# A pooled-attention and expert-choice kernel: the low-part product of each expert's first 256 tokens folded into a 512-column product

## The chip, the cores and the metric

The kernel runs on one core of one Trainium2 chip. The metric is device time in microseconds (us) of one execution; lower is better. Where the text gives a stage or a wait, it comes from one execution taken with the hardware profiler. The engines are called as in the profile: PE is TensorE's multiplication, PEld its weight load, ACT ScalarE, DVE VectorE, POOL GpSimd and SP SyncE, which here issues loads.

## The reference

Attention with pooled keys and values gives 4608 tokens of 512 numbers. Each token then goes to one of 8 experts: tokens and experts are matched greedily by gate value, every expert taking exactly 576 tokens. An expert multiplies by w1 (512 by 1024), takes the maximum with 0, and multiplies by w2 (1024 by 512):

```python
order = np.argsort(-flat)                 # gate values of all tokens and experts
for idx in order:
    tok, e = (int(idx) // E, int(idx) % E)
    if assigned[tok] >= 0 or counts[e] >= cap:
        continue
    assigned[tok] = e
    counts[e] += 1
...
for e in range(E):
    mask = assigned == e
    h = np.maximum(x[mask] @ w1[e], 0.0)
    out[mask] = h @ w2[e]
```

Everything is float32.

## The kernel before, in words

Attention comes first and takes about a quarter of the time; the change does not touch it. Then the experts come one after the other, numbered 0 to 7 here in the order in which they are worked on. While PE works on expert e, the routing (on DVE, with small products on PE) finds the tokens of the expert that comes next, POOL gathers their rows (`xg`, line 1037), and SP loads their weights.

**Products in parts.** PE multiplies float32 numbers in a reduced form, "fp32r". To keep accuracy each factor is cut into a high part and a low part: `high1` (line 1045) copies w1 to `w1h` on ACT, `low1` (line 1049) subtracts on DVE and writes `w1l`; `high2` and `low2` (lines 1055 and 1058) do this for w2, in eight pieces each. Tokens are turned by PE in five tiles of 128, 128, 128, 128 and 64 (`xt`, line 1069, written to PSUM as `tp`); ACT copies the high part `xh` (line 1071) and DVE subtracts to get `xl` (line 1073). A product is then the sum of three: high by high, low by high, high by low.

**Stage 1** (`stage1`) takes the 576 tokens in two parts, the first 256 and the last 320. For each part there are 8 groups, one per 128 columns of w1, called f0 to f7 here. A group is 12 matmuls into one PSUM bank (line 1093): four of w1h by xh, four of w1l by xh, four of w1h by xl. Then ACT writes the high part of the maximum with 0 (`hh`, line 1098), and DVE reads the bank and `hh` and writes the low part (`hl`, line 1101). After that the bank is free. Five banks called `h` go round. Expert 0 takes its parts in halves: f0 to f3 of both parts, then f4 to f7 of both.

**Stage 2** (`products`, line 1127) multiplies hh and hl with w2h and w2l, four tiles of 128 tokens, 24 matmuls of 512 columns each; ACT copies each result to `yt` (line 1141) and POOL scatters its rows to the output (line 1107). The last 64 tokens are multiplied in plain float32 (line 1132), copied to `yh` (line 1145), and scattered as half rows ("halves"). `yh` is a tile of 128 by 256 with two buffers that take turns.

**The order of the work** on every engine is written out by a small planner in `experts` (lines 1202 to 1420). `now` counts PE's time by what the stages yield, `dve` what DVE has been given. `later(after, t, f)` puts DVE work into a list that is written out when `now` has reached the given time; `step` writes one step of the routing; `turn` turns a tile of tokens; `w1.by` and `w2.by` write the pieces of the weights. Each engine then works strictly through its own list. A small product of the routing stands between the large matmuls, at the place where the planner expects its input from DVE: if DVE is later than planned, PE waits there. Expert e+1's first two tiles must be turned before its stage 1 begins.

Of the kernel before, what the change touches and what calls it, by code (L numbers as in the profile page):

```python
# [9 lines left out]
F32 = mybir.dt.float32  # L10
F32R = mybir.dt.float32r
# [3 lines left out]
AF = mybir.ActivationFunctionType  # L15
OP = mybir.AluOpType
# [5 lines left out]
class Attention:  # L22
# [270 lines left out]
    def norm(self, i):  # L293
        c0, c1 = (i // 4 * 4, i // 4 * 4 + 4) if i < self.nt - 4 else (i, i + 1)
        rinv = self.gates(i, c0, c1)
        xt = self.wk.tile([128, 8, 64], F32, name="xt", bufs=8)
        self.nc.vector.tensor_tensor(xt, self.sums_of(i)[:, :, :64], rinv[:, :, None].to_broadcast([128, 8, 64]),
                                     op=OP.mult)
        self.store(i, xt)

    def store(self, i, xt):
        self.nc.scalar.dma_start(self.xd[128 * i:128 * i + 128], xt.rearrange("p h d -> p (h d)"))
# [681 lines left out]
class Experts:  # L984
# [75 lines left out]
    def xt(self, t, name="tp", bufs=2, later=lambda after, t, f: f()):  # L1060

        nc = self.nc
        n = min(128, self.cap - 128 * t)
        if t == 0:
            self.xh = self.buf("xh", [128, 4, 576], F32R)
            self.xl = self.buf("xl", [128, 4, 576], F32R)
        ps = self.psA.tile([128, 4, 128], F32, name=name, bufs=bufs)
        for j in range(4):
            nc.tensor.transpose(ps[:, j, :n], self.xg[:n, t, 128 * j:128 * j + 128], self.ident[:n, :n])  # L1069
        o = slice(128 * t, 128 * t + n)  # L1070
        nc.scalar.activation(self.xh[:, :, o], ps[:, :, :n], AF.Copy)  # L1071
        xl, xh = self.xl[:, :, o], self.xh[:, :, o].bitcast(F32)
        later(1.3, 0.65, lambda: nc.vector.tensor_tensor(xl, ps[:, :, :n], xh, op=OP.subtract))  # L1073

    def stage1(self, later=lambda after, t, f: f(), halves=False, bank=("h", 5)):

        nc = self.nc
        hr = self.buf("hr", [128, 8, 64])
        hh = self.buf("hh", [128, 8, 576], F32R)
        hl = self.buf("hl", [128, 8, 576], F32R)  # L1080
        self.hr, self.hh, self.hl = hr, hh, hl
        cols = slice(0, 256), slice(256, 576)
        for o, some in ((cols[0], range(4)), (cols[1], range(4)), (cols[0], range(4, 8)), (cols[1], range(4, 8))) if (
                halves) else ((cols[0], range(8)), (cols[1], range(8))):
            m = o.stop - o.start
            dt = m / 2400 + 0.017
            for f in some:
                ps = self.psA.tile([128, 512], F32, name=bank[0], bufs=bank[1])
                n = 0
                for a, b in ((self.w1h, self.xh), (self.w1l, self.xh), (self.w1h, self.xl)):  # L1090
                    for j in range(4):
                        fs = slice(128 * f, 128 * f + 128)
                        nc.tensor.matmul(ps[:, :m], a[:, j, fs], b[:, j, o], start=(n == 0), stop=(n == 11))  # L1093
                        n += 1
                        if n < 12:
                            yield dt
                yield dt
                nc.scalar.activation(hh[:, f, o], ps[:, :m], AF.Relu)  # L1098
                if o.start:
                    nc.scalar.activation(hr[:, f], ps[:, 256:320], AF.Relu)  # L1100
                later(0.65, 0.4, lambda f=f, o=o, m=m, ps=ps: nc.vector.scalar_tensor_tensor(  # L1101
                    hl[:, f, o], ps[:, :m], 0.0, hh[:, f, o].bitcast(F32), op0=OP.max, op1=OP.subtract))

    def scatter(self, rows, idx, y):
        nc = self.nc
# [96 lines left out]
def experts(ctx, tc, g, R, xd, w1, w2, out, ident, cap, keep):  # L1202
# [3 lines left out]
    nc = tc.nc  # L1206
    wk = ctx.enter_context(tc.tile_pool(name="moe", bufs=2))
    psB = ctx.enter_context(tc.tile_pool(name="psB", bufs=1, space=PSUM))
    X = Experts(tc, wk, psB, xd, w1, w2, out, ident, cap)

    toks, since, pieces, turned = {}, {}, {}, {}
    held, waiting = [], []

    lows = 0
# [3 lines left out]
    now, dve, ready = 0.0, 0.0, 0.0  # L1218

    def later(after, t, f):  # L1220

        waiting.append((now + after, t, f))

    def flush(left=0):
        nonlocal dve
        while len(waiting) > left:
            due, t, f = waiting.pop(0)
            f()
            dve = max(dve, due) + t
# [33 lines left out]
    def advance(e, t, quiet=False):  # L1263

        nonlocal now, fresh
        now += t
        fresh = False
        while True:
            if waiting and waiting[0][0] <= now:
                flush(len(waiting) - 1)  # L1270
            elif ready > now or quiet or first(e) or not step(e):
                break

    def due(e, what, t):
        return (e, what) in since and now >= since[e, what] + t

    class Pieces:
# [25 lines left out]
    def later_low(after, t, f):  # L1303
# [7 lines left out]
        lows += 1  # L1311
        later(after, t, g)

    def first(e):

        if lows:
            return True
        return e in toks and e in pieces and pieces[e].l < 4 and due(e, "id", 9)

    def turn(e, t, name="tp", bufs=2):  # L1320

        nonlocal now
        now = max(now, since[e, "rows"] + 6.0 + 1.3 * t) + 0.45
        flush(1)
        X.xt(t, name, bufs, later_low)
        turned[e] = t + 1

        if (e, t) == (0, 2):
            later(1.0, 0.2, lambda: X.load_1(behind(0), 2, 4))
        elif (e, t) == (0, 4):  # L1330
            later(1.0, 0.2, lambda: X.load_2(behind(1)))

    def turns(e, upto, late):

        nonlocal last
        t = turned.get(e, 5)
        if t < upto and due(e, "rows", 6.5 + 1.3 * t) and now >= last + 1.4 and (fresh or through or t < late):
            last = now
            turn(e, t)
# [27 lines left out]
    now, ready, dve = 0.0, 0.0, 2.5  # L1367
    last = 0.0
    for e in range(8):
        more = e < 7  # L1370
        if e:
            X.load_2(eids[e])
        w1 = pieces[e]
        w2 = Pieces(e, X.high2, X.low2)
        for n, dt in enumerate(X.stage1(later, not e)):
            k = n if e else n - 48
            if 0 <= k < 48 and n % 2:
                w1.by(4 + (k + 2) // 8)
            if not e and 2 <= n < 96:
                turns(e, 5, 5)  # L1380
            if n == (84 if e else 40):
                for t in range(turned[e], 5):
                    turn(e, t)
            if n >= 64 and n % 2:
                w2.by((n - 70) // 14 if n > 70 else 0)
            if not more and n == 48:
                assert next(g, None) is None
                flag = R.suspect()
                keep()
            elif not more and n == 56:  # L1390
                nc.gpsimd.drain()
            elif not more and n == 136:
                flag = nc.values_load(flag[0:1, 0:1], min_val=0, max_val=1)
            advance(min(e + 1, 7), dt)
            if e and n < 96:
                turns(e, 5, 3 + (n - 14) // 24)
        while w2.l < 8:
            w2.next()
        w1 = pieces[e + 1] = Pieces(e + 1, X.high1, X.low1)
        for n, dt in enumerate(X.stage2(e, *toks[e], range(5 if more else 1))):  # L1400

            advance(min(e + 1, 7), dt, n >= 96)
            if more and due(e + 1, "id", 9):
                w1.by((n - 60) // 12 if n > 60 else 0)
            if more:
                turns(e + 1, 3, (n - 52) // 12)
        if more:
            while e + 1 not in toks:
                now = max(now, ready)
                step(e + 1)  # L1410
            while w1.l < 4:
                w1.next()
            for t in range(turned[e + 1], 2):
                turn(e + 1, t)
        flush(2)
    flush()
    ps = psB.tile([128, 512], F32, name="h", bufs=5)
# [85 lines left out]
```

## Time and profile before

| | us |
|---|---|
| median of 3 runs (612.05 to 612.61) | 612.23 |
| the profiled execution, whole | 612.35 |
| its span, first to last instruction | 609.9 |
| start of stage 1 of expert 0 | 157.1 |
| expert 4: first part of stage 1 | 386.70 to 400.07 |
| expert 4: second part of stage 1 | 400.07 to 415.04 |
| expert 4: stage 2 | 415.04 to 443.26 |

In the views, L1093 is line 1093 of the kernel. A row of a group gives engine, operation, what is written and read, shape and count, then busy time and the mean length of one in ns, then the idle time before it and who ended that. A row of the timeline begins with the start and the length in us. In a row of the windows, each engine's busy time in that stretch is followed by the number of its instructions.

### The profile page before, as it was taken

To read this page: it belongs to the slowest core of one execution; us is meant where nothing else is said; L and a number is where in the kernel's file an instruction comes from. 1 tells how busy PE (TensorE), PEld (TensorE's weight loads), DVE (VectorE), ACT (ScalarE), POOL (GpSimd) and SP (SyncE) were. 2 spreads that over 40 slices of the span, in tenths; PEclk is the share of its full clock that TensorE was granted. 3 is DMA by queue.
4 is the path that set the end of the run, shared out by engine and by line. 5 is a ranking of instruction groups with operands and counts; after the bars stand their busy time and mean duration, and the time that the engine had idled before them with its cause. 6 is when DMAs were issued, how large, how long until landed. Compare 5 with 4: busy or idle time off the path is not lost.

```text
span 609.9 us, 11520 instructions
## 1 busy us (share of the span) xinstructions
PE 591.5 (97%) x4340; PEld 518.3 (85%) x4340; DVE 396.1 (65%) x1164; ACT 240.0 (39%) x562; POOL 177.3 (29%) x222
## 2 busy tenths in 40 slices
PE   8999999985999999999999999999999999999996
PEld 5999999983797799779977987898799889888975
DVE  7578888987885778767964976487367328503500
ACT  7444444461461434233432452255135325513411
POOL 2999999001200500420312301130221123011012
PEclk9999999995999999999999999999999999999999
DMA  8999972223531740616403701540081037014011
GB/s 353 419 420 423 397 274 82 77 100 98 167 116 31 254 147 22 213 62 219 134 35 116 284 1 52 207 174 18 36 323 57 34 120 278 2 52 166 1 40 43
DMA packets 32641, 92.23 MB, mean 151 GB/s; under 512 B 3488, under 2 KB 3488, under 8 KB 29888
## 3 DMA queue, kind: packets, MB, share of 16 engines
q1 hardware_dynamic: 21296, 62.92, 27.5%
q0 software_dynamic: 5952, 19.01, 9.2%
q10 hardware_dynamic: 5328, 9.48, 4.1%
q8 instruction: 35, 0.57, 0.4%
q14 instruction: 30, 0.25, 0.1%
HBM read 72.53 MB, written 18.87 MB: 150 GB/s over the span
## 4 chain that ended last, share of the span: by engine, by line
PE 81%; issue 7%; DVE 4%; DMA 3%; POOL 3%; ACT 1%; SPq 0%; POOLq 0%; ACTq 0%; another core or an unknown queue 0%; DVEq 0%
PE h L1093 32%; PE h L1127 25%; PE psa L272 6%; PE pss L227 5%; PE h L1132 4%; PE tp L1069 3%; DMA rawk<-in_k_dram 2%; PE pse L256 2%; PE rt L256 1%; PE rt L668 1%; DMA out_dram<-yt,rows 1%; PE rt L630 1%; DMA xg<-xd,rows 1%; PE rt L217 1%; DVE e L238 1%
## 5 line engine op out<-in xcount | busy, mean ns | idle before, releaser
L1127 PE MATMUL h<-w2l,hh 128*128 128x512 f32 x256 | 101.8, 398 | 0.0
L1127 PE MATMUL h<-w2h,hh 128*128 128x512 f32 x256 | 101.4, 396 | 0.3 <-PEq L1193 0.3
L1127 PE MATMUL h<-w2h,hl 128*128 128x512 f32 x256 | 101.5, 396 | 0.0
L1107 POOL DMA_INDIRECT out_dram<-yt,rows x29 | 30.3, 1045 | 232.3 <-ACT yt L1141 231.9
L1098 ACT ACTIVATE hh<-h 128x320 fp32r<-128x320 f32 (+1 forms) x128 | 52.5, 410 | 106.6 <-PE h L1093 103.3
L1093 PE MATMUL h<-xh,w1h 128*128 128x320 f32 (+1 forms) x512 | 93.2, 301 | 0.2 <-ACT xh L1071 0.2
L1093 PE MATMUL h<-xl,w1h 128*128 128x320 f32 (+1 forms) x512 | 93.4, 300 | 0.0
L1101 DVE SCALAR_TENSOR_TENSOR hl<-h,hh 128x320 fp32r<-128x320 f32 (+1 forms) x128 | 57.2, 451 | 53.1 <-ACT hh L1098 34.6
L1093 PE MATMUL h<-xh,w1l 128*128 128x320 f32 (+1 forms) x512 | 91.0, 298 | 0.0
L1093 PEld LDWEIGHTS h<-xh,w1h 128*128 128x128 f32 x512 | 75.7, 190 | 3.4 <-issue 2.7
L1093 PEld LDWEIGHTS h<-xl,w1h 128*128 128x128 f32 x512 | 76.1, 190 | 0.4
L1093 PEld LDWEIGHTS h<-xh,w1l 128*128 128x128 f32 x512 | 75.8, 189 | 0.0
L1037 POOL DMA_INDIRECT xg<-xd,rows x40 | 39.3, 982 | 101.9 <-DVE halves L806 52.7
L1141 ACT ACTIVATE yt<-h 128x512 f32<-128x512 f32 x32 | 19.1, 598 | 112.1 <-PE h L1127 67.4
L272 PE MATMUL psa<-vblk,eT 128*128 128x146 f32 (+3 forms) x390 | 59.9, 302 | 0.2
L1127 PEld LDWEIGHTS h<-w2h,hh 128*128 128x128 f32 x256 | 48.2, 188 | 9.3 <-issue 0.7
L1127 PEld LDWEIGHTS h<-w2l,hh 128*128 128x128 f32 x256 | 48.3, 189 | 8.8
L1127 PEld LDWEIGHTS h<-w2h,hl 128*128 128x128 f32 x256 | 48.2, 188 | 8.8
L272 PEld LDWEIGHTS psa<-vblk,eT 128*128 128x128 f32 (+1 forms) x390 | 50.9, 180 | 1.8 <-issue 0.3
L1049 DVE TENSOR_TENSOR w1l<-raw,w1h 128x512 fp32r<-128x512 f32 x64 | 41.7, 685 | 13.4 <-ACT w1h L1045 13.1
L1073 DVE TENSOR_TENSOR xl<-tp,xh 128x512 fp32r<-128x512 f32 (+1 forms) x40 | 25.3, 633 | 37.4 <-ACT xh L1071 37.3
L1058 DVE TENSOR_TENSOR w2l<-raw,w2h 128x512 fp32r<-128x512 f32 x64 | 43.2, 682 | 2.0 <-ACT w2h L1055 1.8
(224 smaller groups left out, 903.3 us busy)
## 6 DMA issues: line engine op xcount, KB each, us to landing
raw<-in_moe_w_dram SPq DMA_DIRECT2D x64, 512.0 KB, 6.3
xd<-xt ACTq DMA_DIRECT2D x36, 256.0 KB, 5.6
rawv<-in_v_dram SPq DMA_DIRECT2D x7, 1280.0 KB, 14.1
rawk<-in_k_dram SPq DMA_DIRECT2D x7, 1152.0 KB, 11.7
rawq<-in_q_dram SPq DMA_DIRECT2D x7, 1152.0 KB, 11.8
rawk<-in_k_dram SPq DMA_DIRECT2D x2, 576.0 KB, 4.7
rawv<-in_v_dram SPq DMA_DIRECT2D x1, 768.0 KB, 8.0
rawq<-in_q_dram SPq DMA_DIRECT2D x1, 640.0 KB, 9.0
```

The lines of the kernel that those rows point to most:

```text
L227: nc.tensor.matmul(ps[cols, j // 2, 144 * (j % 2):144 * (j % 2) + 144], self.q_of(b, j, n, cols.stop - cols.start), self.kblk[b % 4][:, j] ...
L272: self.nc.tensor.matmul(o[h], self.eT[i][:, c, h], self.vblk[b % 4][:, self.BLOCKS[c]:self.BLOCKS[c + 1]], start=(c == cs[0]), stop=(c == ...
L1037: nc.gpsimd.indirect_dma_start(out=self.xg[:n, t, :], out_offset=None, in_=self.xd, in_offset=bass.IndirectOffsetOnAxis(ap=rows[:n, t:t + ...
L1049: self.nc.vector.tensor_tensor(l, raw, h.bitcast(F32), op=OP.subtract)
L1058: self.nc.vector.tensor_tensor(self.w2l[:, i], self.raw2[e][:, i], self.w2h[:, i].bitcast(F32), op=OP.subtract)
L1073: later(1.3, 0.65, lambda: nc.vector.tensor_tensor(xl, ps[:, :, :n], xh, op=OP.subtract))
L1093: nc.tensor.matmul(ps[:, :m], a[:, j, fs], b[:, j, o], start=(n == 0), stop=(n == 11))
L1098: nc.scalar.activation(hh[:, f, o], ps[:, :m], AF.Relu)
L1101: later(0.65, 0.4, lambda f=f, o=o, m=m, ps=ps: nc.vector.scalar_tensor_tensor(hl[:, f, o], ps[:, :m], 0.0, hh[:, f, o].bitcast(F32), op0= ...
L1107: st = nc.gpsimd.indirect_dma_start(out=rows, out_offset=bass.IndirectOffsetOnAxis(ap=idx, axis=0), in_=y, in_offset=None)
L1127: nc.tensor.matmul(ps, a[:, f, o], b[:, f], start=(f == 0 and k == 0), stop=(f == 7 and k == 2))
L1132: nc.tensor.matmul(ps[64 * a:64 * a + 64, :256], self.hr[:, f], self.raw2[e][:, f, 256 * a:256 * a + 256], start=(f == 0), stop=(f == 7))
```

## The change

In the first 256 tokens' part, the high and the low part of x now stand side by side in one tile, `xa`, with 4 by 2 by 256 columns; the other 320 tokens are in `xb`. A group of the first part is 8 matmuls instead of 12 (`first`): four of w1l by the high part, 256 columns, then four of w1h by high and low side by side, 512 columns. The bank's left half then holds w1l by xh plus w1h by xh, its right half w1h by xl. The halves are added afterwards: ACT copies the right half to a tile called `yh`, DVE adds it to the left half in place, ACT takes the maximum with 0 (`hh`), and DVE makes `hl` as before. The second part (`second`) does what it did.

Since the 5th matmul of the first group already reads the low part, `lowered` writes out the subtraction of x's low parts ahead of it.

```diff
@@ xt
+            self.xa = self.buf("xa", [128, 4, 2, 256], F32R)
+            self.xb = self.buf("xb", [128, 2, 4, 320], F32R)
...
+        xh, xl = (self.xa[:, :, i, o] if t < 2 else self.xb[:, i, :, o] for i in range(2))
+        nc.scalar.activation(xh, ps[:, :, :n], AF.Copy)
+        later(1.3, 0.65, lambda: nc.vector.tensor_tensor(xl, ps[:, :, :n], xh.bitcast(F32), op=OP.subtract))
@@ stage1
-                for a, b in ((self.w1h, self.xh), (self.w1l, self.xh), (self.w1h, self.xl)):
-                    for j in range(4):
-                        fs = slice(128 * f, 128 * f + 128)
-                        nc.tensor.matmul(ps[:, :m], a[:, j, fs], b[:, j, o], start=(n == 0), stop=(n == 11))
...
+                yield from (self.second if o.start else self.first)(f, o, ps, later, ready)
+
+    def first(self, f, o, ps, later, ready):
...
+        for j in range(4):
+            nc.tensor.matmul(ps[:, :256], self.w1l[:, j, fs], self.xa[:, j, 0], start=(j == 0), stop=False,
+                             skip_group_check=True)
+            yield 0.12
+        if f == 0:
+            ready()
+        for j in range(4):
+            nc.tensor.matmul(ps, self.w1h[:, j, fs], self.xa[:, j].rearrange("p v c -> p (v c)"), start=False,
+                             stop=(j == 3), skip_group_check=True)
+            yield 0.1135
+            yield 0.1135
+        part, whole = self.wk.tile([128, 256], F32, name="yh", bufs=2), ps[:, :256]
+        nc.scalar.activation(part, ps[:, 256:], AF.Copy)
+
+        def add():
+            nc.vector.tensor_tensor(whole, whole, part, op=OP.add)
+            nc.scalar.activation(hh, whole, AF.Relu)
+            later(0.65, 0.4, lambda: nc.vector.scalar_tensor_tensor(hl, whole, 0.0, hh.bitcast(F32), op0=OP.max,
+                                                                    op1=OP.subtract))
+
+        later(0.65, 0.4, add)
@@ experts
+    def lowered():
+        while lows:
+            flush(len(waiting) - 1)
...
-        for n, dt in enumerate(X.stage1(later, not e)):
+        for n, dt in enumerate(X.stage1(later, not e, ready=lowered)):
```

The planner writes everything in another order with this, on all engines. Three places matter here. In these rows "waits" names the counters that the instruction waits for: those called DMASW count the landing of transfers that POOL issued.

**ACT at the start of expert 7.** Before, from the copy of the scattered half rows (L1145, or L1170 after) on:

```order
L1145 ACTIVATE yh<-h 128x256 [waits PE_49]
L1071 ACTIVATE xh<-tp 128x4x128 [waits PE_49]
L1071 ACTIVATE xh<-tp 128x4x64 [waits PE_49]
L1098 ACTIVATE hh<-h 128x256 [waits DVE_49,PE_49]
L1098 ACTIVATE hh<-h 128x256 [waits PE_49] x4
```

After:

```order
L1170 ACTIVATE yh<-h 128x256 [waits PE_49]
L1072 ACTIVATE xb<-tp 128x4x128 [waits PE_49]
L1072 ACTIVATE xb<-tp 128x4x64 [waits PE_49]
L1105 ACTIVATE yh<-h 128x256 [waits PE_49]
L1109 ACTIVATE hh<-h 128x256 [waits DVE_49]
L1105 ACTIVATE yh<-h 128x256 [waits DMASW4_49,PE_49,Activation_49]
L1109 ACTIVATE hh<-h 128x256 [waits DVE_49]
L1105 ACTIVATE yh<-h 128x256 [waits PE_49,Activation_49]
```

Each group now has two instructions on ACT instead of one, and the second group's copy waits for a transfer that POOL issued: the copies share the two buffers of `yh` with the half rows that are being scattered.

**DVE in the first part of expert 7**, where one small step of the routing's last test (L892) stands among the groups. Before:

```order
L1073 TENSOR_TENSOR xl<-tp,xh 128x4x128 [waits Activation_49]
L1073 TENSOR_TENSOR xl<-tp,xh 128x4x64 [waits Activation_49]
L1101 SCALAR_TENSOR_TENSOR hl<-h,hh 128x256 [waits Activation_49] x3
L892 TENSOR_SCALAR rc<-bad 128x1
L895 TENSOR_SCALAR flag<-rt 1x1 [waits PE_49]
```

After:

```order
L1108 TENSOR_TENSOR h<-h,yh 128x256 [waits DVE_49,Activation_49]
L1110 SCALAR_TENSOR_TENSOR hl<-h,hh 128x256 [waits Activation_49]
L1108 TENSOR_TENSOR h<-h,yh 128x256 [waits Activation_49]
L1110 SCALAR_TENSOR_TENSOR hl<-h,hh 128x256 [waits Activation_49]
L1108 TENSOR_TENSOR h<-h,yh 128x256 [waits Activation_49]
L1110 SCALAR_TENSOR_TENSOR hl<-h,hh 128x256 [waits Activation_49]
L892 TENSOR_SCALAR rc<-bad 128x1
L895 TENSOR_SCALAR flag<-rt 1x1 [waits PE_49]
```

The step stands behind three groups, as before, but each is now an addition and a subtraction, and both wait for ACT. On PE the product that reads `rc` (L894) stands behind the first matmul of f4 in both kernels.

**DVE at the start of expert 2**, the last pieces of the weights' low part (L1049). Before, they stand ahead of all of the expert's groups:

```order
L1049 TENSOR_TENSOR w1l<-raw_3295,w1h 128x512 [waits DMAHW3_49]
L1049 TENSOR_TENSOR w1l<-raw_3295,w1h 128x512 [waits Activation_49]
L672 TENSOR_TENSOR diagc<-rt,dq 128x32 [waits PE_49]
L676 TENSOR_REDUCE cnt<-diagc 128x8 [waits DVE_49]
L1073 TENSOR_TENSOR xl<-tp,xh 128x4x128 [waits Activation_49]
L687 TENSOR_TENSOR g_247<-rt,need_3469 32x8 [waits PE_49]
L1073 TENSOR_TENSOR xl<-tp,xh 128x4x64 [waits Activation_49]
L1101 SCALAR_TENSOR_TENSOR hl<-h,hh 128x256 [waits Activation_49]
```

After:

```order
L1108 TENSOR_TENSOR h<-h,yh 128x256 [waits Activation_49]
L1110 SCALAR_TENSOR_TENSOR hl<-h,hh 128x256 [waits Activation_49]
L625 TENSOR_TENSOR cmp<-q16a,j_196 128x1152 [waits DVE_49]
L1108 TENSOR_TENSOR h<-h,yh 128x256 [waits Activation_49]
L1110 SCALAR_TENSOR_TENSOR hl<-h,hh 128x256 [waits Activation_49]
L1049 TENSOR_TENSOR w1l<-raw_3370,w1h 128x512
L1108 TENSOR_TENSOR h<-h,yh 128x256 [waits Activation_49]
```

The eighth piece now stands behind the additions and subtractions of f0 and f1. PE reads it in the fourth matmul of f4.

More of the change, by code (lines that the diff above doesn't have):

```diff
@@ L1064, in xt @@
         if t == 0:
-            self.xh = self.buf("xh", [128, 4, 576], F32R)
-            self.xl = self.buf("xl", [128, 4, 576], F32R)
+            self.xa = self.buf("xa", [128, 4, 2, 256], F32R)
+            self.xb = self.buf("xb", [128, 2, 4, 320], F32R)
         ps = self.psA.tile([128, 4, 128], F32, name=name, bufs=bufs)
@@ L1069, in xt, with stage1 @@
             nc.tensor.transpose(ps[:, j, :n], self.xg[:n, t, 128 * j:128 * j + 128], self.ident[:n, :n])
[L1070 to L1075, printed above, removed]
+        o = slice(128 * (t % 2), 128 * (t % 2) + 128) if t < 2 else slice(128 * t - 256, 128 * t - 256 + n)
+        xh, xl = (self.xa[:, :, i, o] if t < 2 else self.xb[:, i, :, o] for i in range(2))
+        nc.scalar.activation(xh, ps[:, :, :n], AF.Copy)
+        later(1.3, 0.65, lambda: nc.vector.tensor_tensor(xl, ps[:, :, :n], xh.bitcast(F32), op=OP.subtract))
+    def stage1(self, later=lambda after, t, f: f(), halves=False, bank=("h", 5), ready=lambda: None):
         nc = self.nc
@@ L1084, in stage1 @@
                 halves) else ((cols[0], range(8)), (cols[1], range(8))):
-            m = o.stop - o.start
-            dt = m / 2400 + 0.017
             for f in some:
                 ps = self.psA.tile([128, 512], F32, name=bank[0], bufs=bank[1])
-                n = 0
-                for a, b in ((self.w1h, self.xh), (self.w1l, self.xh), (self.w1h, self.xl)):
-                    for j in range(4):
-                        fs = slice(128 * f, 128 * f + 128)
[L1093 to L1102, printed above, removed]
+                yield from (self.second if o.start else self.first)(f, o, ps, later, ready)
@@ new lines, in first @@
+    def first(self, f, o, ps, later, ready):
+        nc, hh, hl = self.nc, self.hh[:, f, o], self.hl[:, f, o]
+        fs = slice(128 * f, 128 * f + 128)
+        for j in range(4):
[17 more added lines that the diff above has]
+        later(0.65, 0.4, add)
@@ new lines, in second @@
+    def second(self, f, o, ps, later, ready):
+        nc, hh, hl = self.nc, self.hh[:, f, o], self.hl[:, f, o]
+        fs = slice(128 * f, 128 * f + 128)
+        for n, (a, b) in enumerate(((self.w1h, 0), (self.w1l, 0), (self.w1h, 1))):
+            for j in range(4):
+                nc.tensor.matmul(ps[:, :320], a[:, j, fs], self.xb[:, b, j], start=(n == j == 0),
+                                 stop=(n == 2 and j == 3))
+                yield 0.15
+        nc.scalar.activation(hh, ps[:, :320], AF.Relu)
+        nc.scalar.activation(self.hr[:, f], ps[:, 256:320], AF.Relu)
+        later(0.65, 0.4, lambda: nc.vector.scalar_tensor_tensor(hl, ps[:, :320], 0.0, hh.bitcast(F32), op0=OP.max,
+                                                                op1=OP.subtract))
```

## The prediction, as it was put on record

> **What bounds the kernel now.** First the page: its span, the engines' busy time and the chain that ended last.
>
> ```profile
> span 609.9 us, 11520 instructions
> PE 591.5 (97%) x4340; PEld 518.3 (85%) x4340; DVE 396.1 (65%) x1164; ACT 240.0 (39%) x562; POOL 177.3 (29%) x222
> PE 81%; issue 7%; DVE 4%; DMA 3%; POOL 3%; ACT 1%; SPq 0%; POOLq 0%; ACTq 0%; another core or an unknown queue 0%; DVEq 0%
> ```
>
> PE is busy in 97% of the span and holds 81% of the chain: less work on PE shortens the time, a new wait on PE lengthens it. DVE has 35% to spare, but an average hides the stages. So next the windows (length, then busy time of PE, PEld, DVE, ACT, POOL, then PE's granted clock): expert 0's halves of 256 and of 320 tokens, expert 4's first part, second part and stage 2, and expert 7's first part.
>
> ```profile
> 157.12:171.79 14.67, 14.67 (x117) 14.37 (x118) 13.38 (x44) 7.74 (x19) 0.00 (x0) 1.00 0.60 210
> 171.79:185.40 13.61, 13.61 (x111) 13.22 (x110) 10.98 (x32) 6.89 (x19) 0.00 (x0) 1.00 0.05 20
> 386.70:400.07 13.37, 13.37 (x127) 13.11 (x126) 9.84 (x36) 4.81 (x12) 3.52 (x4) 1.00 0.90 322
> 400.07:415.04 14.97, 14.97 (x118) 14.56 (x117) 13.12 (x36) 7.54 (x22) 2.37 (x4) 1.00 0.25 83
> 415.04:443.26 28.22, 28.22 (x166) 21.17 (x164) 13.96 (x45) 8.80 (x17) 4.78 (x8) 1.00 0.10 38
> 552.23:565.13 12.90, 12.90 (x107) 12.55 (x106) 6.27 (x17) 6.46 (x15) 1.06 (x2) 1.00 0.50 176
> ```
>
> PE never stands still in any of them. DVE is where room is short: expert 0 has 1.29 and 2.63 us of it, expert 4's first part 3.53, its second part 1.85, its stage 2 14.26. The change adds DVE work just in the first parts.
>
> **What PE saves.** The timeline (start, length) gives PE's pace. Twelve matmuls of 256 columns lie between the starts of the first two rows, twelve of 512 columns between the other two:
>
> ```profile
> 387.28 0.64 PE L1093 MATMUL h<-xh,w1l 128*128 128x256 f32 x4
> ...
> 388.71 0.64 PE L1093 MATMUL h<-xh,w1l 128*128 128x256 f32 x4
> 305.12 0.39 PE L1127 MATMUL h<-w2h,hh 128*128 128x512 f32 x1
> ...
> 307.84 0.39 PE L1127 MATMUL h<-w2h,hh 128*128 128x512 f32 x1
> ```
>
> That is 1.43/12 = 0.1192 us and 2.72/12 = 0.2267 us each. A group was 12 x 0.1192 = 1.430 and becomes 4 x 0.1192 + 4 x 0.2267 = 1.384 us; 64 groups save 64 x 0.046 = 3.0 us. The Trainium skill, "TensorE: Matmul & The Clock Gate", section "Wait — 56ns, not 53.3ns?", gives a warm pace of columns / 2.4 GHz plus about 2.5 ns; by it two narrow matmuls exceed a wide one by only 2.5 ns, the whole saving would be about 0.6 us and the time 2.4 us later. The trace disagrees: its narrow matmul takes 12.5 ns over 106.7. I take the trace.
>
> **What is added.** Each group gains a copy on ACT and an addition on DVE. Nearest are these groups (busy, mean ns) and this pair of the timeline:
>
> ```profile
> L1098 ACT ACTIVATE hh<-h 128x256 fp32r<-128x256 f32 x64 | 24.5, 383 | 47.9 <-PE h L1093 46.1 <-PE rt L694 1.6
> L1101 DVE SCALAR_TENSOR_TENSOR hl<-h,hh 128x256 fp32r<-128x256 f32 x64 | 26.2, 416 | 34.8 <-ACT hh L1098 34.6
> L1073 DVE TENSOR_TENSOR xl<-tp,xh 128x512 fp32r<-128x512 f32 x32 | 22.0, 687 | 35.9 <-ACT xh L1071 35.8
> 388.43 0.38 ACT L1098 ACTIVATE hh<-h 128x256 fp32r<-128x256 f32 x1 [1.23 <-PE h L1093]
> 388.85 0.42 DVE L1101 SCALAR_TENSOR_TENSOR hl<-h,hh 128x256 fp32r<-128x256 f32 x1 [10.61 <-ACT hh L1098]
> ```
>
> The copy has L1098's shape: 0.383 us, 24.5 us in all; it lies beside PE. The addition I take at 0.42, L1101's size (not under 0.38, which ACT takes for as many columns; not over the 0.687 of twice the columns): 27 us in all. ACT hands to DVE in 388.85 - 388.81 = 0.04 us. A group's chain on DVE is then addition 0.42, ACT's maximum 0.38 with two hand-offs, subtraction 0.42: 1.30 us against PE's 1.384, as DVE stands waiting for the maximum in program order. It keeps up, with almost nothing over; the routing, the weight pieces and `xl` all queue behind.
>
> **The new wait.** The copies share the two buffers of `yh` with the half rows that are scattered. So ACT's second group copy of experts 1 to 7 (f1, in experts 3 and 6 f2) waits for that scatter's landing. The view of the tile `yh`, the DMA issues, and expert 7's timeline show when that is:
>
> ```profile
> L1145 ACT ACTIVATE yh<-h x8: 383/383/385, 214.9 to 605.4; 128x256 f32<-128x256 f32 x8
> DMA to landing us min/median/max: 2.4/6.3/6.7
> out_dram<-yt,rows POOLq DMA_INDIRECT x29, 2.8
> out_dram<-yh,halves POOLq DMA_INDIRECT x7, 6.3
> 552.34 0.97 SPq L1028 DMA_DIRECT2D raw<-in_moe_w_dram  x2
> 552.35 0.38 ACT L1145 ACTIVATE yh<-h 128x256 f32<-128x256 f32 x1 [2.97 <-PE h L1132]
> 553.00 0.97 POOL L1107 DMA_INDIRECT out_dram<-yh,halves  x1 [2.29 <-ACT yh L1145]
> ```
>
> With S the start of the expert's stage 1 (552.23), POOL issues at S+0.8 and the rows land 6.3 us after: S+7.1, since w2's load goes out beside it (552.34). The other scatters take 2.8. PE has finished f1 at S + 2 x 1.384 = 2.8, and the copy could start at 3.0: ACT is blocked for about 4.1 us, then DVE at f1's addition, and all that stands behind both. Counted on from 7.1 with 0.04 to 0.07 a hand-off: copy f1 until 7.5, addition 7.95, maximum 8.4, subtraction f1 8.85, addition f2 9.3, its maximum 9.7, subtraction f2 10.2. PE has banks for f0 to f4 and runs on; it stops where a small product or weight piece is late. Costs of what stands there:
>
> ```profile
> L1049 DVE TENSOR_TENSOR w1l<-raw,w1h 128x512 fp32r<-128x512 f32 x64 | 41.7, 685 | 13.4 <-ACT w1h L1045 13.1 <-DMA raw<-in_moe_w_dram 0.3
> L625 DVE TENSOR_TENSOR cmp<-q,j 128x1152 bf16<-128x1152 f16 x18 | 13.7, 759 | 0.6
> L1071 ACT ACTIVATE xh<-tp 128x512 fp32r<-128x512 f32 x32 | 19.1, 598 | 33.9 <-PE tp L1069 33.9
> 389.62 0.64 PE L1069 MATMUL tp<-ident,xg 128*128 128x128 f32 x4
> 390.01 0.37 PE L1093 MATMUL h<-xl,w1h 128*128 128x256 f32 x1
> ```
>
> - Expert 7: `rc` (L892) stands behind f2's subtraction: ready at 10.4. PE wants it (L894) after four groups, two turned tiles (390.01 - 389.62 = 0.39 each) and one matmul: 5.5 + 0.8 + 0.1 = 6.5. Stall 3.9.
> - Expert 2: the last `w1l` piece stands behind f1's subtraction: 8.85 + 0.685 = 9.6 with the hand-off. PE reads it in f4's fourth matmul, after one turned tile and some small products: 6.6. Stall 3.0.
> - Expert 4: the product L694 in f4 needs `g`, behind f1's subtraction and a half tile's `xl` (estimate 0.41, by L1101's columns): 9.4 against PE's 8.0, stall 1.4; the next (L668) behind one more group pair, about 1.5. Together 2.9.
> - Expert 5: L668 in f4 needs `cmp`, behind f1's subtraction and two small steps: 8.85 + 0.4 + 0.76 = 10.0 against 7.8; with smaller ones 2.8.
> - These four: 12.6 us. Experts 1, 3, 6 and the second parts that inherit the late DVE: their copy waits too, but I find no early reader; between 0 and 6, and I take 2.
> - Expert 0 has no scatter before it. Its halves get 4 x (0.42 + 0.43 waiting) = 3.4 us each of DVE time in 1.29 and 2.63 us of room: 2.1 + 0.8 = 3, up to 5 if the later halves repeat it.
> - Expert 1's turned tiles stand now behind the last product of expert 0's stage 2, with no matmul between: PE waits for ACT (0.60) and `xl` (0.687), less half a microsecond of narrow matmuls and turning: 1.5, between 0.7 and 2.
>
> Long stalls also touch PE's clock, as these rows show, the end of the kernel and the time before expert 0:
>
> ```profile
> 601.68 3.67 PE L1132 MATMUL h<-raw,hr 128*64 128x256 f32 x32
> 607.00:608.00 1.00, 0.00 (x0) 0.00 (x0) 0.00 (x0) 0.00 (x0) 0.03 (x1) 0.95 0.36 131
> 608.00:609.00 1.00, 0.00 (x0) 0.00 (x0) 0.00 (x0) 0.00 (x0) 0.00 (x0) 0.50 0.01 0
> 151.05 2.72 PE L526 MATMUL h<-ones 128*128 128x512 bf16 x6
> 153.00:154.00 1.00, 0.94 (x3) 0.17 (x2) 1.00 (x3) 0.56 (x2) 0.96 (x1) 0.53 0.64 139
> ```
>
> PE's last matmul ended at 605.35, the clock fell to half at 607.9: 2.55 us idle. Dense work from 151.05 brought it back at 153.94, after 2.9 us, in which half the work is lost: 1.45 us. Expert 7's stall of 3.9 should pay that once: 1.5 (0, if it is shorter; 3, if expert 2's pays too). The Trainium skill, same page, section "What's actually happening", has the clock fall after an idle window of about 3.4 us that runs free of the kernel; by it a stall of 3.9 holds a whole window in one case of seven, and the sum would be about 1.3 us lower. One ending cannot decide between them; the row is nearer.
>
> **Sum:** 12.6 + 2 + 3 + 1.5 + 1.5 - 3.0 = +17.6. The profiled execution took 612.35, 609.9 of it span; 629.95 follows, and the median of the runs lies 0.12 lower: 629.8. The terms' own ends give some 620 to 638.
>
> **The rivals.**
> - *The saving wins (faster).* All the stalls hang on the landing. If the half rows land as the other scatters do (2.8, or the view's minimum of 2.4, in place of 6.3), at S+3.6 rather than S+7.1, ACT is blocked for 0.6 us and the chain of 1.30 fits under 1.384; if the free banks then also hide the 4.5 us at experts 0 and 1, what is left is 612.35 - 3.0 - 0.1 = 609.3. The point is a landing before about S+4.2: 2.9 earlier than I have it, the stalls of 3.9, 3.0, 2.9 and 2.8 become 1.0, 0.1, 0 and 0. For it: nothing else is short there. Against: seven of seven half-row scatters lie near 6.3, and the load beside them stays. 0.10.
> - *They cancel.* Stalls of 2 to 4 us in all, if my reading of where PE stops is off nearly everywhere: about 612. 0.05.
> - *Only some places stall:* one or two of the four and half of expert 0's: 614 to 620. 0.10.
> - *DVE becomes the bound of stage 1.* Per expert 0 to 5: 9.84 + 13.12 = 22.96 busy, plus 8 x 0.42 added, 8 x 0.46 standing between addition and subtraction, 4.5 idle in the ring wait: 34.5 against PE's 28.0 (13.0 + 15.0). Six times 6.5 is 39, less the 3.0 saved 36: 648. Against: a late DVE catches up in stage 2, with 14 us of room. 0.10.
>
> **How the numbers follow.** The forecast has 0.65. Low 611 takes in cancelling, high 642 the forecast's upper end and a mild form of the last rival; left out are the saving (0.10) and most of the last (under 0.10). About 0.2%, 1.2 us, is what a measurement of this kernel can tell from no change: faster 0.10, same 0.05, slower 0.65 + 0.10 + 0.10 = 0.85.
>
> **What would show it.** In the profile after: idle time of about 4 us on ACT ahead of L1105, ended by the `halves` scatter, in seven experts; PE idle at L894 in expert 7 for about 3.9 us with a clock below 1.00 behind it; PE waits at `w1l` in expert 2 and at L694 and L668 in experts 4 and 5; DVE busy up by about 27 us, ACT by 24.5; in undisturbed groups 1.384 us from group to group. It is wrong if ACT shows no such wait; if the wait is there and PE runs through; or if the groups themselves come at DVE's pace, 1.4 us or more with DVE never idle.

## The result, and the profile after the change

| | before | after |
|---|---|---|
| median of 6 runs each, us | 611.80 (611.39 to 612.61) | 629.84 (627.71 to 632.98) |
| the profiled execution, whole, us | 612.35 | 627.71 |
| its span, us | 609.9 | 625.5 |

The changed kernel takes 1.0301 times as long (95% interval 1.0269 to 1.0333): it is slower. The profiled execution happens to be the fastest of its six, and the six lie within 5.3 us of each other where the kernel before stays within 1.2. Both points come back below.

The page of the changed kernel, the same three lines as of before:

```profile
span 625.5 us, 11183 instructions
PE 594.6 (95%) x4084; PEld 503.6 (81%) x4084; DVE 421.2 (67%) x1228; ACT 255.9 (41%) x626; POOL 178.7 (29%) x222
PE 48%; issue 22%; DVE 14%; POOL 6%; DMA 5%; ACT 4%; POOLq 0%; ACTq 0%; DVEq 0%; another core or an unknown queue 0%
```

PE's share of the chain falls from 81% to 48%, and DVE, POOL, DMA and ACT come into it: PE now waits for others. Which others, the view of PE's waits says (in total us, times, the longest); these six lines stand in it and not in before's, or not so large:

```profile
PE rt L779 <- DVE OHa L769: 3.3, 2, 2.3
PE h L1094 <- DVE w1l L1049: 3.0, 2, 2.4
PE rt L894 <- DVE rc L892: 2.4, 1, 2.4
PE rt L668 <- DVE cmp L625: 1.7, 4, 0.9
PE rt L694 <- DVE g L687: 1.7, 4, 1.0
PE h L1094 <- issue: 1.1, 1, 1.1
```

(One wait of 2.3 in the first line was there before, ahead of expert 0. The last line is the start of expert 1, at 216.91, just behind ACT's copies of the turned tiles.) The two longest new waits are where the prediction has them: the last `w1l` piece in expert 2 (2.35) and `rc` in expert 7 (2.38). The longest for `cmp` (0.95) is in expert 5, as forecast; that for `g` (0.99) is in expert 3, not in 4. Behind them stands the new group, here the groups by line and form (busy, mean ns, idle before it and who ended that):

```profile
L1105 ACT ACTIVATE yh<-h 128x256 f32<-128x256 f32 x64 | 24.4, 381 | 21.7 <-DMA out_dram<-yh,halves 10.3 <-PE h L1100 9.7 <-PE rt L694 1.7
L1108 DVE TENSOR_TENSOR h<-h,yh 128x256 f32<-128x256 f32 x64 | 27.1, 423 | 17.4 <-ACT yh L1105 17.4
L1109 ACT ACTIVATE hh<-h 128x256 fp32r<-128x256 f32 x64 | 24.6, 385 | 59.9 <-DVE h L1108 58.2 <-DVE w2l L1058 1.7
L1110 DVE SCALAR_TENSOR_TENSOR hl<-h,hh 128x256 fp32r<-128x256 f32 x64 | 27.1, 424 | 25.8 <-ACT hh L1109 25.3 <-issue 0.5
```

The copy takes 381 ns and the addition 423, as estimated. ACT sits idle 10.3 us for the scatter of the half rows, in five experts and never longer than 3.2, and DVE stands for ACT's maximum in the groups' chains, 25.3 us in all. The timeline of expert 7 (start 565.55) shows how one leads to the other:

```profile
566.32 0.97 POOL L1132 DMA_INDIRECT out_dram<-yh,halves  x1 [2.29 <-ACT yh L1170]
569.17 0.39 ACT L1109 ACTIVATE hh<-h 128x256 fp32r<-128x256 f32 x1 [0.50 <-DVE h L1108]
...
571.90 0.39 ACT L1105 ACTIVATE yh<-h 128x256 f32<-128x256 f32 x1 [2.34 <-DMA out_dram<-yh,halves]
572.32 0.43 DVE L1108 TENSOR_TENSOR h<-h,yh 128x256 f32<-128x256 f32 x1 [2.30 <-ACT yh L1105]
...
574.76 0.15 DVE L892 TENSOR_SCALAR rc<-bad 128x1 bf16<-128x1 f32 x1
574.96 0.16 PE L894 MATMUL rt<-ones,rc 128*1 128x1 bf16 x1 [2.38 <-DVE rc L892]
```

The rows land some 5.5 us after POOL's issue, f1's copy starts at once, `rc` follows 2.9 us later, and PE has stood 2.38 us.

From the start of one expert's stage 1 to the next one's (expert 7: to the last tile's plain products), from the timelines of both kernels:

| expert | 0 | 1 | 2 | 3 | 4 | 5 | 6 | 7 |
|---|---|---|---|---|---|---|---|---|
| before, us | 57.62 | 57.69 | 57.73 | 56.54 | 56.56 | 54.36 | 54.61 | 49.45 |
| after, us | 59.46 | 59.50 | 60.13 | 58.73 | 57.90 | 57.87 | 54.51 | 51.64 |
| more | +1.84 | +1.81 | +2.40 | +2.19 | +1.34 | +3.51 | -0.10 | +2.19 |

Expert 6 alone gains, and it is the one where PE waits nowhere over 0.12 us. The loss is spread more evenly than forecast. A part of the differences is work that moved: the routing's small products are 405 in these stretches in both kernels, but experts 1 and 2 have 22 fewer each than before, and experts 3, 4 and 5 have 9, 12 and 23 more.

### The profile page after: what moved, and what is told of

It is laid out like the page before. It is cut to its first block, busy times and chain, and to the rows that moved or that the text cites. A ratio compares the mean times of both kernels' runs of the same rounds, so it can differ in the third digit from the quotient of the medians.

```text
span 625.5 us, 11183 instructions
## 1 busy us (share of the span) xinstructions
PE 594.6 (95%) x4084; PEld 503.6 (81%) x4084; DVE 421.2 (67%) x1228; ACT 255.9 (41%) x626; POOL 178.7 (29%) x222
## 4 chain that ended last, share of the span: by engine, by line
PE 48%; issue 22%; DVE 14%; POOL 6%; DMA 5%; ACT 4%; POOLq 0%; ACTq 0%; DVEq 0%; another core or an unknown queue 0%
PE h L1152 16%; PE h L1121 7%; PE psa L272 7%; PE pss L227 5%; POOL xg L1037 3%; DMA out_dram<-yh,halves 3%; POOL out_dram L1132 2%; PE h L1100 2%; DVE h L1108 2%; DVE hl L1110 2%; ACT hh L1109 2%; PE h L1157 2%; PE pse L256 2%; PE h L1094 1%; PE tp L1069 1%
## 5 line engine op out<-in xcount | busy, mean ns | idle before, releaser
L1121 PE MATMUL h<-xb,w1h 128*128 128x320 f32 x512 | 89.7, 312 | 0.2 <-DVE late L1380 0.2
L1121 PEld LDWEIGHTS h<-xb,w1h 128*128 128x128 f32 x512 | 78.4, 188 | 1.6 <-ACT xb L1072 0.5
L1100 PE MATMUL h<-xa,w1h 128*128 128x512 f32 x256 | 72.8, 401 | 0.0
L1037 POOL DMA_INDIRECT xg<-xd,rows x40 | 42.1, 1052 | 60.9 <-DVE halves L806 42.7
L1121 PE MATMUL h<-xb,w1l 128*128 128x320 f32 x256 | 50.1, 313 | 0.0
L1094 PE MATMUL h<-xa,w1l 128*128 128x256 f32 x256 | 45.7, 292 | 4.1 <-DVE w1l L1049 3.0
L1109 ACT ACTIVATE hh<-h 128x256 fp32r<-128x256 f32 x64 | 24.6, 385 | 59.9 <-DVE h L1108 58.2
L1094 PEld LDWEIGHTS h<-xa,w1l 128*128 128x128 f32 x256 | 39.3, 190 | 11.8 <-issue 3.7
L1100 PEld LDWEIGHTS h<-xa,w1h 128*128 128x128 f32 x256 | 43.4, 189 | 5.4 <-issue 0.2
L1049 DVE TENSOR_TENSOR w1l<-raw,w1h 128x512 fp32r<-128x512 f32 x64 | 41.6, 687 | 8.4 <-ACT w1h L1045 6.1
L1110 DVE SCALAR_TENSOR_TENSOR hl<-h,hh 128x256 fp32r<-128x256 f32 x64 | 27.1, 424 | 25.8 <-ACT hh L1109 25.3
```

Source lines behind the costliest of these rows:

```text
L1037: nc.gpsimd.indirect_dma_start(out=self.xg[:n, t, :], out_offset=None, in_=self.xd, in_offset=bass.IndirectOffsetOnAxis(ap=rows[:n, t:t + ...
L1049: self.nc.vector.tensor_tensor(l, raw, h.bitcast(F32), op=OP.subtract)
L1094: nc.tensor.matmul(ps[:, :256], self.w1l[:, j, fs], self.xa[:, j, 0], start=(j == 0), stop=False, skip_group_check=True)
L1100: nc.tensor.matmul(ps, self.w1h[:, j, fs], self.xa[:, j].rearrange("p v c -> p (v c)"), start=False, stop=(j == 3), skip_group_check=True)
L1109: nc.scalar.activation(hh, whole, AF.Relu)
L1110: later(0.65, 0.4, lambda: nc.vector.scalar_tensor_tensor(hl, whole, 0.0, hh.bitcast(F32), op0=OP.max, op1=OP.subtract))
```

## The experiments

Three explanations compete. **A**: the wait for the scatter's landing, as the prediction has it. **B**: the added work on DVE and its standing for ACT. **C**: the order, since the planner counts the new groups and so puts routing products and turned tiles at other places.

**A tile of their own for the copies.**

```diff
-        part, whole = self.wk.tile([128, 256], F32, name="yh", bufs=2), ps[:, :256]
+        part, whole = self.wk.tile([128, 256], F32, name="part", bufs=2), ps[:, :256]
```

> The copies get a tile of their own (two buffers), so none waits for a scatter; nothing else differs, the order on every engine is the changed kernel's. Theory A, the wait for the scatter's landing costs most: ACT's five waits for it (10.3 us) vanish, and with them PE's waits at w1l in expert 2 (2.35), at L694 and L668 in expert 3 (1.28), at L668 in expert 5 (0.95) and at L894 in expert 7 (2.38), each with some 0.25 of starting again: about 8 of the 18 us, and the 2 us by which the median stands above the profiled execution if the clock is behind it: 618 to 622. Rival B, the added work on DVE and its waiting for ACT is what delays PE, and the scatter's wait only hides it: 626 or more. Rival C, the altered order of the routing's products: 626 or more as well.

Measured: 620.97 (618.94 to 621.59), 1.0153 times before (1.0136 to 1.0170). The groups of ACT's copy and DVE's addition:

```profile
L1105 ACT ACTIVATE part<-h 128x256 f32<-128x256 f32 x64 | 24.4, 381 | 10.2 <-PE h L1100 9.8
L1108 DVE TENSOR_TENSOR h<-h,part 128x256 f32<-128x256 f32 x64 | 27.0, 422 | 8.0 <-ACT part L1105 7.8
```

The scatter is gone from the idle time. The shared tile costs 629.84 - 620.97 = 8.9 us, half of the loss, as A said; but 9.1 are left, so B or C, or both, hold too.

**Matmuls and order alone.** Neither copy nor addition is written; the planner's step for the addition stays and holds ACT's maximum.

```diff
-        nc.scalar.activation(part, ps[:, 256:], AF.Copy)
...
-            nc.vector.tensor_tensor(whole, whole, part, op=OP.add)
```

> The changed kernel's matmuls and its order, but neither copy nor addition: the product of w1's high part with x's low part is left out of the first 256 tokens' result. Theory A and rival B both: with nothing added on ACT and DVE the waits of PE inside stage 1 vanish; left are the late turned tiles at experts 1 and 2 (1.1 and 0.7 us), and PE's saving of 1.3 to 3.0: 610 to 613. Rival C, the order itself makes PE wait: 618 or more.

Measured: 616.26 (613.70 to 616.77), 1.0075 times before (1.0058 to 1.0092). Not 610 to 613, and not 618 either: with no work added to ACT or DVE the kernel is 4.4 us slower. The timeline at the end of expert 0 and the start of expert 1 shows one reason, at the end of expert 1 another (the two rows that stand alone are the kernel before's at the end of expert 1):

```profile
213.62 1.09 PE L1069 MATMUL tp<-ident,xg 128*128 128x128 f32 x8
215.95 0.74 PE L1094 MATMUL h<-xa,w1l 128*128 128x256 f32 x4 [1.24 <-ACT xa L1072]
...
268.81 0.65 PE L1069 MATMUL tp<-ident,xg 128*128 128x128 f32 x4
269.40 1.51 PE L1155 MATMUL h<-raw,hr 128*64 128x256 f32 x12
270.84 0.66 PE L1069 MATMUL tp<-ident,xg 128*128 128x128 f32 x4
271.43 1.52 PE L1155 MATMUL h<-raw,hr 128*64 128x256 f32 x12
272.88 0.66 PE L1069 MATMUL tp<-ident,xg 128*128 128x128 f32 x4
273.46 0.65 PE L1155 MATMUL h<-raw,hr 128*64 128x256 f32 x4
274.05 0.74 PE L1094 MATMUL h<-xa,w1l 128*128 128x256 f32 x4
```

```profile
268.82 3.67 PE L1132 MATMUL h<-raw,hr 128*64 128x256 f32 x32
272.43 0.38 PE L1093 MATMUL h<-xh,w1h 128*128 128x256 f32 x1
```

At expert 1 both tiles are turned after the last product and PE stands 1.24 us for their copy. Ahead of expert 2 three tiles now stand among the plain float32 products of the last 64 tokens. Those products took 3.6 us without tiles (268.82 to 272.43 before) and take 5.82 with three (268.23 to 274.05): 0.74 a tile, where the prediction's rows have 0.39 for a tile among the narrow matmuls of stage 1. So a moved tile costs 0.35 with no wait in any view. The wait and the three tiles make 2.3 us.

**The same matmuls with nearly before's order.** The planner counts as before, but for 0.15 instead of 0.1503 a matmul in the second parts.

```diff
-            yield 0.12
+            yield 0.1237
...
-            yield 0.1135
-            yield 0.1135
+            yield 0.1237
+            yield 0.1237
...
-        later(0.65, 0.4, add)
+        nc.scalar.activation(hh, whole, AF.Relu)
+        later(0.65, 0.4, lambda: nc.vector.scalar_tensor_tensor(hl, whole, 0.0, hh.bitcast(F32), op0=OP.max,
+                                                                op1=OP.subtract))
```

> Matmuls of the changed kernel without copy and addition (the product of w1's high part with x's low part is left out of the first 256 tokens' result), and the planner counting as before the change (0.1237 a matmul, one step of 0.4 on DVE for a group), so that the order is nearly that of before. If the 4.4 us that the matmuls alone cost with the new order come from the order (late turned tiles and routing products), this is faster than before by PE's saving, 0.26 an expert as the undisturbed experts 6 and 7 showed: 609 to 610.2; by the prediction's 3.0 it would be 608.8. If the wide matmuls themselves cost it, or if the planner's numbers don't matter: 614 or more.

Measured: 610.19 (609.60 to 611.01) against 611.68 in the same session, 0.9972 (0.9962 to 0.9982). The wide products with their order nearly as before are worth 1.5 us. One tile has moved all the same: expert 0 turns two among its plain products, before one. A run below in which expert 0 multiplies as before has this too, and its expert 0 takes 0.29 us more than before; without it the saving is an estimated 1.8. And the changed order costs 616.26 - 610.19 = 6.1 us: C holds. The two places above explain at most 2.3 of them. The profile of that run is of its fastest execution, 613.70, and 2.6 below its median, so where the rest arises is not shown.

**The wait alone, in the kernel before.** One copy a group on ACT that nobody reads, once into the shared tile and once into one of its own:

```diff
                 yield dt
+                if not o.start:
+                    nc.scalar.activation(self.wk.tile([128, 256], F32, name="yh", bufs=2), ps[:, :256], AF.Copy)
                 nc.scalar.activation(hh[:, f, o], ps[:, :m], AF.Relu)
```

> The kernel before, with its twelve matmuls and its order, and one copy of each first group on ACT into the shared tile (nobody reads it). Theory A: f1's copy waits for the landing in experts 1 to 7, ACT's maximum and DVE's subtraction stand behind it; in expert 7 rc comes at about 9.3 us after the start of stage 1 where PE wants it at 7.1, so 2.2 us there, and 1 to 2 us in two or three others: 615 to 620. Rivals B and C (the wait alone is harmless): 611 to 613.

> As the run with copies in the kernel before, but into a tile of their own. All theories: 24.5 us more on ACT beside PE, no wait: 611.3 to 612.8. A rival on the copy itself (reading the bank while DVE wants it, or ACT too full): 614 or more.

Measured: 618.00 (617.50 to 620.82) with the shared tile, 1.0116 (1.0090 to 1.0142); 611.85 (611.45 to 613.38) with its own, 1.0004 (0.9995 to 1.0014). The two kernels differ in a tile's name. The copies' group with the shared tile:

```profile
L1099 ACT ACTIVATE yh<-h 128x256 f32<-128x256 f32 x64 | 24.7, 386 | 51.3 <-PE h L1093 31.3 <-DMA out_dram<-yh,halves 15.2 <-PE tp L1069 2.1
```

And with a tile of their own:

```profile
L1099 ACT ACTIVATE part<-h 128x256 f32<-128x256 f32 x64 | 24.6, 384 | 43.6 <-PE h L1093 38.8 <-remote 1.8 <-issue 1.6
```

With their own tile 24.6 us more on ACT cost nothing; with the shared one, ACT's 15.2 us of idle time before the scatter's landing come to 6.2 us of the whole. That is A without any of the rest.

**DVE not standing for ACT.** On top of the copies' own tile, ACT takes `hh` from the left half at once, and DVE adds and subtracts in one go.

```diff
+        nc.scalar.activation(hh, whole, AF.Relu)
 
         def add():
             nc.vector.tensor_tensor(whole, whole, part, op=OP.add)
-            nc.scalar.activation(hh, whole, AF.Relu)
-            later(0.65, 0.4, lambda: nc.vector.scalar_tensor_tensor(hl, whole, 0.0, hh.bitcast(F32), op0=OP.max,
-                                                                    op1=OP.subtract))
+            nc.vector.scalar_tensor_tensor(hl, whole, 0.0, hh.bitcast(F32), op0=OP.max, op1=OP.subtract)
 
-        later(0.65, 0.4, add)
+        later(1.1, 0.85, add)
```

> As the run with a tile of their own for the copies, but ACT takes hh from the left half at once and DVE's addition and subtraction follow each other; the planner counts 0.85 for both in one step. Theory: of the 4.7 us between the run without copy and addition (616.3) and the one with its own tile (621.0) most is DVE standing for ACT's maximum; it goes: 616 to 618. Rival, DVE's added 27 us: 620 to 621.

Measured: 616.36 (616.04 to 616.83), 1.0075 (1.0060 to 1.0090). The groups on DVE, first with the own tile alone, then in this run:

```profile
L1110 DVE SCALAR_TENSOR_TENSOR hl<-h,hh 128x256 fp32r<-128x256 f32 x64 | 27.1, 424 | 25.7 <-ACT hh L1109 25.7
```

```profile
L1109 DVE TENSOR_TENSOR h<-h,part 128x256 f32<-128x256 f32 x64 | 27.2, 425 | 10.6 <-ACT hh L1106 10.3
L1110 DVE SCALAR_TENSOR_TENSOR hl<-h,hh 128x256 fp32r<-128x256 f32 x64 | 27.2, 425 | 2.2
```

DVE is as busy, its idle time ahead of the subtraction falls from 25.7 to 2.2 us, and the whole by 4.6, down to the time of the run that had no copy and no addition. So B's standing for ACT may be what cost, rather than its work. It is not shown alone: the order changed with the planner's new step as well, and a run below moves the time by 2.8 us with the planner's counts and nothing else.

**The same with nearly before's order.** The planner counts 0.1237 a matmul and 0.4 on DVE for a group, as if nothing had been added.

> A whole kernel with three differences from the changed one: the copies have their own tile, the planner counts as before the change, and ACT takes hh from the left half at once, so that DVE adds and subtracts without standing for ACT (hl takes up the difference). DVE still gets 27 us more. Theory: the wait for ACT in the chain and the order are what was left besides the scatter, so this comes near before: 610 to 613, with what DVE's additions cost in expert 0 and in the second parts (1 to 3 us) against PE's saving of 2.1. Rival: DVE's added time as such is the limit: 616 or more.

Measured: 616.75 (616.41 to 618.77), 1.0098 (1.0080 to 1.0116): outside the 610 to 613 expected, and the rival's side. PE's waits name the place:

```profile
PE rt L668 <- DVE cmp L625: 3.5, 3, 1.6
```

Before's order leaves DVE no time for the additions in the second parts of experts 3 and 4, where PE stands 1.65 and 1.56 us for `cmp`. So the 27 us on DVE do have a price: either as waits in the old order, or as the planner's later places in the new one. Against the run without copy and addition in the old order it is 616.75 - 610.19 = 6.6 us here and 616.36 - 610.19 = 6.2 us in the run before. Half of the 6.6 is these two waits (3.2 us); the rest is open.

**Only the planner's clock.** As the run in which DVE doesn't stand, with 0.1237 for each of twelve steps in place of 0.12 and 0.1135:

> As the run in which ACT takes hh at once, with the planner's step of 0.85 on DVE for a group, but with before's 0.1237 a matmul in place of 0.12 and 0.1135. If the planner's clock, which runs 0.1 us a group ahead of the narrow matmuls' count, matters, this differs from 616.4 by over 1 us; if only the DVE time that it counts sets the order's cost, 615.5 to 617.

Measured: 613.53 (612.47 to 615.20), 1.0035 (1.0025 to 1.0046): 2.8 us better by a number in the planner that is, if anything, less true to PE's pace. That is over the 1 us that was set beforehand as the sign that PE's count matters: the order's cost is not set by DVE's count alone. The price of the additions is 613.53 - 610.19 = 3.3 us in this order. Two waits at expert 1 (0.90 and 0.71 us) are left in stage 1 of experts 0 to 6, counting those over 0.12 us.

**Only where room is.** Two whole kernels, each with the copies' own tile and without the standing; the other experts multiply as before.

> A whole kernel: experts 0 to 5 multiply as before the change, only 6 and 7, beside which no routing or nearly none is left, use the wide products, with the copies in their own tile, ACT's hh taken at once and the planner counting as before. Theory: each of the two first parts gets 0.26 us shorter and nothing waits: 0.5 us faster than before, 611.2, at the edge of what can be measured. Rival: DVE's additions delay something there too, at L894 above all: 612 to 613.

Measured: 612.15 (611.53 to 613.52), 1.0013 (1.0004 to 1.0022): no gain. In expert 7 the one wait of PE eats the saving, in expert 6 the first part took 13.42 us after 13.36. The most is lost where nothing was widened: expert 0 takes 57.91 us after 57.62, with a second tile turned among its plain products. The two tiles, and the wait:

```profile
210.46 0.66 PE L1069 MATMUL tp<-ident,xg 128*128 128x128 f32 x4
...
212.49 0.66 PE L1069 MATMUL tp<-ident,xg 128*128 128x128 f32 x4
...
559.71 0.16 PE L894 MATMUL rt<-ones,rc 128*1 128x1 bf16 x1 [0.21 <-DVE rc L892]
```

> A whole kernel: wide products in experts 1 to 6 alone, copies in their own tile, ACT's hh taken at once, the planner counting 0.1237 a matmul and 0.85 on DVE for a group; expert 0, where DVE has least room, and expert 7, where L894 waits, multiply as before. In the run with all eight experts so, PE's two waits at the start of expert 1 (0.90 and 0.71 us) came from the late turned tiles; with expert 0 as before they go: 613.5 - 1.6 - 0.5 = 611.4, no different from before, or 1 faster at most. Rival: the routing's later places in experts 3 to 5 (0.9, 0.4 and 0.3 us there) decide, and the tiles stay late: 612.5 to 613.5.

Measured: 610.82 (609.69 to 612.70) against 611.73, 0.9983 (0.9972 to 0.9993): 0.9 us faster than before, by an interval that just excludes no change, and under the 1.2 us that the prediction counted as telling. It is the only whole kernel here below the one before. In its stages 1 and 2 PE waits nowhere over 0.12 us for DVE, ACT or a DMA. First parts of experts 5 and 6 take 13.10 us, 0.26 less than before.

**The changed kernel once more**, for a slower execution's profile.

> The changed kernel once more, for its profile. Its six runs lie between 627.7 and 633.0 where the kernel before stays within 1.2 us. If a halved clock after a long stall makes the difference, a slower execution shows a stage with a granted clock below 1.00 and a stall of more than 2.5 us just before it; if the landing of the gathered rows or of the scatter varies, it shows longer waits for these at a clock of 1.00. A profile near 627.7 decides nothing.

It took 632.72, 5.0 us more than the first profile. Windows of one us in expert 7 (length, busy time of PE, PEld, DVE, ACT, POOL, PE's granted clock, and last the DMA engines' share and GB/s), and its timeline:

```profile
577.00:578.00 1.00, 0.00 (x0) 0.00 (x0) 0.55 (x3) 0.49 (x2) 0.00 (x0) 1.00 0.17 61
579.00:580.00 1.00, 1.00 (x5) 0.81 (x4) 0.55 (x2) 0.38 (x1) 0.09 (x1) 0.50 0.00 0
581.00:582.00 1.00, 1.00 (x5) 0.92 (x5) 0.03 (x1) 0.97 (x3) 0.00 (x0) 0.50 0.00 0
582.00:583.00 1.00, 1.00 (x5) 0.81 (x4) 1.00 (x2) 0.45 (x1) 0.00 (x0) 0.80 0.02 8
...
578.47 0.16 PE L894 MATMUL rt<-ones,rc 128*1 128x1 bf16 x1 [2.14 <-DVE rc L892]
579.02 1.91 PE L1100 MATMUL h<-xa,w1h 128*128 128x512 f32 x4
```

After a stall of 2.14 us PE's clock is halved from 579.0, half a microsecond after PE went on, to about 582.4, and expert 7's first part takes 16.41 us where the first profile has 15.11, at 1.00 throughout and after a longer stall (2.38). Expert 2 shows the same (a stall of 2.19, then 0.50 for 3.4 us, 16.82 against 15.53). With the stalls themselves some 0.2 shorter, a fall cost about 1.5 us, and the two parts hold 2.6 of the 5.0; 1.9 more are in expert 1's first part (15.10 against 13.21), where the clock is 1.00 and PE stands 1.13 us for ACT's `xb`. That copy stands on ACT behind the group copies, and f1's waits longer for the scattered half rows, here in the first profile (start of stage 1 at 216.91) and in this one (217.23):

```profile
223.70 0.39 ACT L1105 ACTIVATE yh<-h 128x256 f32<-128x256 f32 x1 [3.17 <-DMA out_dram<-yh,halves]
```

```profile
225.91 0.38 ACT L1105 ACTIVATE yh<-h 128x256 f32<-128x256 f32 x1 [4.95 <-DMA out_dram<-yh,halves]
```

It starts 6.79 us after the start of stage 1 in the one and 8.68 in the other. So the difference between these two executions has two sources, the clock and when the half rows land.

## Why the prediction was right, point by point

The time, 629.8 against 629.84, agrees better than its terms do. The direction, the shared tile as the largest cause, most of its places and the rise on ACT and DVE were right; four sizes were off and made up for each other, and that the total agrees so closely is luck.

- **PE's saving, 3.0 us: mis-sized.** It is 1.5, by the run with nearly before's order and no additions, or an estimated 1.8 without the tile that moved there. A group takes 1.40 us in undisturbed stretches, not 1.384, which by itself would save 64 x 0.03 = 1.9:

```profile
569.49 0.63 PE L1094 MATMUL h<-xa,w1l 128*128 128x256 f32 x4
569.96 1.09 PE L1100 MATMUL h<-xa,w1h 128*128 128x512 f32 x4
570.89 0.64 PE L1094 MATMUL h<-xa,w1l 128*128 128x256 f32 x4
```

  The four wide matmuls take 0.93, 0.2325 each, where stage 2's take 0.2267: a row of another stage was carried over. Why they are slower here was not settled. By the Trainium skill ("TensorE: Matmul & The Clock Gate", "Wait — 56ns, not 53.3ns?") the saving would have been an estimated 0.6; the measurement lies between that and mine.
- **The wait for the landing, 14.6 us with experts 1, 3 and 6: mis-sized.** Taking it away gives 8.9, and 6.2 in the kernel before. The prediction had ACT idle about 4 us in each of seven experts; the view has 10.3 us in five, 3.2 at most (1.7 before expert 5's copy, which it puts down to L694, may belong to them). The rows came sooner than at S+7.1 (f1's copy began at S+6.35 in expert 7, S+6.94 in expert 2), and PE came later to its places (at S+7.0 rather than 6.5 and 6.6). Expert 7 stood 2.38 rather than 3.9, expert 2 2.35 rather than 3.0, experts 4 and 5 far less than 2.9 and 2.8; expert 3 stood (0.99 and 0.29), for which I had found no reader. With a tile of their own for the copies, 0.41, 0.51 and 0.52 and 0.28 are left in experts 7, 2 and 3, so not all of these stalls was the landing's. That the load of w2 beside it makes the landing late, as the prediction has it, no run here tests.
- **DVE's added work, 3 us in expert 0: mis-sized and misplaced.** Copy and addition cost 620.97 - 616.26 = 4.7 in all, in the same order. By the two profiles expert 0 has 59.60 - 58.52 = 1.1 of it, and experts 1 to 5, where the prediction has none, 0.4 to 1.2 each. How much of it is DVE's standing for ACT is not shown apart from the order. The chain of 1.30 in 1.384 was read rightly: it keeps up, and what queues behind it is late.
- **The turned tiles at expert 1, 1.5 us: right there, short in all.** The wait was 1.12 us. What I left out is that every routing product and tile moves with the planner's count: the order costs 6.1 us where I had 1.5.
- **The clock, 1.5 us: right in kind.** The first profile shows no halved clock behind a stall, the second shows it twice, at about 1.5 us each; it helps to explain why the median stands 2 us over the first profile. It is not all of that: one execution took 629.82 at the same mean granted clock, 0.984, as the first profile's. The Trainium skill's idle window of about 3.4 us (same page, "What's actually happening") does not fit: 2.14 and 2.19 us of standstill were enough once, 2.38 were not another time.
- **The rivals.** That the saving wins once nothing waits for the landing is refuted: with the copies' own tile the kernel is still 1.5% slower. DVE as the bound of stage 1 at 648 is refuted too; the waits of PE for DVE that the profile of the changed kernel has in the experts all stand in stage 1, so what is late is caught up in stage 2, as argued. The other two, about 612 and 614 to 620, are ruled out by the time, and the waits stand at more places than they allow.

In sum: -1.5 for the products, +6.1 for the order, +4.7 for copy and addition, +8.9 for the shared tile: 18.2, where 18.0 was measured. These are differences along one chain of runs, so they add up of themselves and the sum proves nothing. In another order of steps the sizes differ: the shared tile cost 6.2 in the kernel before, and the additions 3.3 to 6.6 over the run without them in other orders.

## What to carry to other kernels

A tile's name is a resource: reusing `yh` tied a group copy on ACT in most experts, and all that stood behind it, to a transfer, and a new name alone gave half the loss back. When an order is written out by a planner, price the change of the order apart from the work, by running the new instructions with the old counts and the other way round; here the order weighed 6.1 against a saving of 1.5. And a total that comes out right is no proof of its terms: each needs its own run.

## What the runs showed of the hardware

- PE's granted clock fell to 0.50 for about 3.4 us after standstills of 2.14 and 2.19 us in one execution, and stayed at 1.00 after one of 2.38 in another; each fall cost about 1.5 us.
- The scattered half rows landed at different times in two executions of one kernel: in expert 1 the copy that waits for them began 6.79 us after the start of stage 1 in one and 8.68 in the other.
- Turning a tile of 128 tokens cost PE 0.74 us among plain float32 matmuls and 0.39 among the reduced ones.
- A copy on ACT of the first 256 tokens' 64 banks, 24.6 us of it, cost the kernel nothing (1.0004, 0.9995 to 1.0014).
